# Cosine attention on one core: a second fold of the sums on GpSimd, and a new plan of loads and order

## The chip, the core and the metric

The kernel runs on one core of one Trainium2 chip. The core has TensorE (matmuls into PSUM), VectorE and ScalarE (both read PSUM and SBUF), GpSimd [...], and SyncE, which in this kernel issues nearly all transfers, one after the other, in the order of its program. Times are device microseconds of a whole execution. A page of the profile shows one execution; its span runs from the first to the last instruction. In the profile PE is TensorE, PEld its loads of stationary operands, DVE is VectorE, ACT ScalarE, POOL GpSimd, SP SyncE; SPq is SyncE's issuing of transfers.

## The reference

Attention with normalized queries and keys and one temperature for each head: 1 batch, 32 heads, 2048 positions, 20 elements a head, bfloat16.

```python
def reference(q, k, v, t):
    eps = 1e-6
    qn = q / (jnp.sqrt((q * q).sum(axis=-1, keepdims=True)) + eps)
    kn = k / (jnp.sqrt((k * k).sum(axis=-1, keepdims=True)) + eps)
    logits = jnp.einsum('bhqd,bhkd->bhqk', qn, kn) * t[None, :, None, None]
    attn = _softmax(logits, axis=-1)
    return jnp.einsum('bhqk,bhkd->bhqd', attn, v)
```

For each head 2048 x 2048 exponentials are needed, 134 million in all, and two matmuls with a depth or a width of only 20.

## The kernel before, in words

**Tiles.** The 2048 keys of a head are 16 row tiles of 128. For one row tile, TensorE makes the logits of 128 keys against all 2048 queries in four matmuls of 512 queries (`qk_mm`, line 758). Since the depth is 20, the queries of the four groups of 512 sit in four strips of 32 partitions, and the keys must be there in four rotations: `qkT` is the transposed tile, `kR` holds its three rotations, `qz` the queries, each in its own strip.

**Two ways to an exponential.** A row tile goes one of two ways. On way A, ScalarE computes the exponential from PSUM (`psA`) to `p_ring`, in waves of 2 and 3 units of 512 in turn (line 849; a unit is 128 keys by 512 queries). On way D, VectorE writes a scaled and shifted integer whose bits are a rough exponential (`xt`, line 905, two pieces of 1024 a row tile, both through the one buffer `psD`), and three more integers with 256, 512 and 768 added (`ss`, lines 912 and 916, called shifts here). The four, each with its own scaled copy of v (`vph`, line 574, made by GpSimd), average the error out. `DVE_TILES` says how many row tiles of each head go by way D; before, 157 of 512, and 355 by way A. A shift is either one VectorE instruction of 2048 int16 or GpSimd adds on pieces of it, seen as int32 (1024 words a shift). The products with v (line 778) add up in `psO`; the row sum comes from a column of ones in `vaug`. At the head's end VectorE transposes `psO` (line 791), takes the reciprocal, GpSimd multiplies (line 802), SyncE stores.

**Preparation of a head** (`add_loads`, `add_prep`, `add_trn`): SyncE loads k, q (four pieces) and v. VectorE squares (line 604), from head 3 on GpSimd adds the two halves of each row of 20 squares (`fold`, line 612, 320 elements a head), VectorE sums the rest (`rs_sum`, line 619) and finds the reciprocal root in five small steps (lines 623 to 635), multiplies the query half with the temperature (line 641). GpSimd normalizes (`qkn`, line 653; VectorE for heads 1 and 2). SyncE then issues a transposing transfer (line 671), which waits for that, four transfers into `qz` and six into `kR`. From head 5 on, two heads are prepared together. Only when `qz` and `kR` have landed can TensorE begin with the head.

**What sets the order.** A planner written in Python (`Program`) holds every instruction as a task with an engine, an assumed cost, a priority and its predecessors, and lists each engine's order once, when the program is built. On the chip each engine goes through its list, and waits for semaphores[...]. GpSimd's pieces are put into stretches in which VectorE runs an instruction of line 905, a reduction or a transpose (`pool_fill`, `win`). `schedule` lists anew up to `PASSES` times and chooses how many rows of the array a logit matmul uses (32, 64 or 128 partitions), to keep a measure of TensorE's activity above `LOAD`. `SWITCH` is an amount that a task of another kind on TensorE is put back by; `DSL` adds to the estimate of when VectorE is free; `SPARE` bounds which matmuls may be made wider. `LEAD` is how many heads ahead preparation is due, `SPREAD` how far its steps are set apart. `DLEAD` sets way D of a head 0.75 of a head ahead of way A. Three buffers (`NT`) hold transposed heads, so the transpose of head h waits until the logits of head h − 3 are made.

The DMA tasks have two costs in the planner: `dur`, how long SyncE's queue takes to issue one (0.65 if nothing is said), and `lat`, how long until it lands.

Of the kernel before, what the change touches and what calls it, by code (L numbers as in the profile page):

```python
# [45 lines left out]
class Program:  # L46
# [2 lines left out]

    SEM_LAT = {"PE": 0.20, "ACT": 0.30, "DVE": 0.14, "POOL": 0.15, "SP": 0.0}  # L50

    SWITCH = 0.1
    LIGHT = 9.0
    TICK = 3.41
    LOAD = 3550.0
    PASSES = 16
    FIRM = 8
    MARGIN = 600.0
    PE_REST = 4.2
# [2 lines left out]
    PRATE = 0.00164  # L62
    KEEP = 0.3
    RESTP = 0.3
    SPARE = 0.05
    DSL = 0.0
    HOLDA = 1.0
    HPE = 0.2
    HDV = 0.02
# [75 lines left out]
    def list_schedule(self):  # L145
# [39 lines left out]
        def leave(t, now):  # L185

            for u in t.users:
                lat = t.lat if t.dma else (
                    self.SEM_LAT[t.eng] if u.eng != t.eng else 0.12 if t.eng == "DVE" else 0.0)
                if u.eng == "PE" and u.name[:2] == "pv":  # L190
                    lat += self.PV_SLACK
                rt[u.seq] = max(rt[u.seq], t.end + lat)
                u.n -= 1
                if u.n == 0:
                    arrive(u, max(now, rt[u.seq]))
# [64 lines left out]
        while events or ready["POOL"]:  # L260
# [6 lines left out]
            while events and events[0][0] <= now:  # L267
                _, kind, _, t = heapq.heappop(events)
# [5 lines left out]
            for e in touched:  # L274
# [14 lines left out]
                if e == "PE":  # L289
# [8 lines left out]
                    t = x[2]  # L298
                elif e == "POOL":
# [3 lines left out]
                    t = x[2]  # L303
                else:
                    _, _, t = heapq.heappop(ready[e])
# [28 lines left out]
    def plan_waits(self):  # L334
        pos = {}
        for e, ts in self.order.items():
            for i, t in enumerate(ts):
                pos[t.seq] = i
        for t in self.tasks:
            for d in t.deps:  # L340
                if not d.dma and (d.eng != t.eng or d.eng == "DVE" or t.name == "qt0"):
                    d.inc = True
        dma_cnt = {}
        for e, ts in self.order.items():
            c = 0
            for t in ts:
                if t.dma:
                    dma_cnt[t.dma] = dma_cnt.get(t.dma, 0) + 16
                    t.cnt = dma_cnt[t.dma]
                elif t.inc:  # L350
                    c += 1
                    t.cnt = c
        allt = sorted(self.tasks, key=lambda t: (t.start, pos[t.seq]))
        known = {e: {} for e in self.order}
        snap = {}
        waits = {}
        for t in allt:
            kn = known[t.eng]
            need = {}
            for d in t.deps:  # L360
                if not d.dma and d.eng == t.eng and d.eng != "DVE" and t.name != "qt0":
                    continue
                key = d.dma if d.dma else d.eng
                if need.get(key, (0, None))[0] < d.cnt:
                    need[key] = (d.cnt, d)
            ws = []
            for key, (c, d) in sorted(need.items(), key=lambda kv: -kv[1][1].end):
                if kn.get(key, 0) >= c:
                    continue
                ws.append((key, c))  # L370
                kn[key] = c
                for k2, c2 in snap[d.seq].items():
                    if kn.get(k2, 0) < c2:
                        kn[k2] = c2
            waits[t.seq] = ws
            snap[t.seq] = dict(kn)
        self.waits = waits
# [12 lines left out]
def bass_standalone__qk_norm__prompt_kernel(  # L390
# [16 lines left out]
    NB = 8  # L407
# [8 lines left out]
    NWARM = 14  # L416
    EARLY = 3
    NSOLO = 3
    LEAD = 3.0
    SPREAD = 0.4  # L420
    FIRST = -7.0
    DLEAD = 0.75
    PE_MM = 0.23
    MORE = 12
    DLM = 2
    DVE_TILES = [4, 4, 4, 5, 4, 5, 5, 5, 5, 5, 5, 5, 5, 5, 6, 5, 6, 5, 5, 5, 5, 3, 5, 5, 5, 4, 5, 6, 6, 5, 5, 5]
    NDMAX = 6
    NPOOL, FPOOL = True, True
    FUSE, FOLD = True, 1
    NQ, NSQ, NSTEP = 2, 4, 0.0  # L430
    EXP0 = 0.051
    RSPOOL = False
    TTRATE = 0.00168
    TTDUR, TTWIN = 0.8, 0.55
    NCH = 1

    with ExitStack() as es:
# [14 lines left out]
        rs = {x: sbuf(f"rs_{x}", [128, 2 * NQ * R], F32) for x in ("sum", "u", "a", "b", "y", "r")}  # L452
# [19 lines left out]
        def dma(eng, name, dst, src, deps, pri, key, lat=2.2, dur=0.65):  # L472
            return add(eng, name, lambda e, tk: e.dma_start(dst, src), dur, deps, pri, lat=lat, dma=key)  # L473
# [59 lines left out]
        tcp = add("ACT", "tcp", lambda e, tk: e.activation(t_f32[:, :], tb16[:, :], ACT.Copy), 0.2, [ld_t], -90.85)  # L533


        lds, ld_v, norm, trn, rot = {}, {}, {}, {}, {}
# [14 lines left out]
        def add_loads(h):  # L551
            b, bv = (h + 1) % NB, h % NV
            pri = h - LEAD - 0.5
            war = (norm[h - NB] if h >= NB else []) + ([lambda: [trn[max(h - 3, 0) if h < 5 else h - 4]]] if h >= EARLY else [])
            x = qk_of(h)
            lds[h] = [dma("SP", f"ldk{h}", x[:, R:2 * R, :], k[0, h].rearrange("(p r) d -> p r d", p=128),
                          war, pri - 0.01 if h else -50, f"k{b}", lat=4.5 if h else 2.2)]
            if h == 0:
                lds[h].append(dma("ACT", "ldq0", x[:, 0:R, :], q[0, 0].rearrange("(p r) d -> p r d", p=128),
                                  [], -99, "q0a"))  # L560
            else:

                for nh in range(4):
                    src = bass.AP(q.tensor, q[0, h].offset + nh * D,
                                  [[16 * D, 32], [4 * D, 4], [512 * D, 4], [1, D]])
                    dst = x[32 * nh:32 * nh + 32, 0:R, :].rearrange("p (c g) d -> p c g d", g=4)
                    lds[h].append(dma("SP", f"ldq{h}", dst, src, war, pri, f"q{b}", lat=4.5))
            war = (pv_users[h - NV] if h >= NV else z_v[bv]) + ([lambda: [trn[h - 2]]] if h >= 2 else [])
            if h == 1:
                war = war + [lambda: [trn[0]]]  # L570
            ld_v[h] = dma("SP", f"ldv{h}", vaug[bv][:, :, 0:D], v[0, h].rearrange("(p r) d -> p r d", p=128),
                          war, pri + 0.1, f"v{bv}", lat=3.0)
            nd = 4 if h < DLM else DVE_TILES[h]
            vsc[h] = [add("POOL", f"vs{h}", lambda e, tk, i=i: e.tensor_scalar(  # L574
                vph[bv][:, i, 0:nd, :], vaug[bv][:, R - nd:R, :], 2.0 ** (-PHASES[i] / 1024.0), 1.0, ALU.mult, ALU.mult),
                0.4, [ld_v[h]] + (pv_users[h - NV] if h >= NV else z_v[bv]), pri + 0.2) for i in range(len(PHASES))]
            for u in vsc[h] if h else []:
                u.win = 0.14

        def add_prep(hs):  # L580
            due = hs[0] - LEAD if hs[0] != 1 else FIRST
            n = len(hs)
# [9 lines left out]
            def pool(name, fn, win, deps):  # L592
                step[0] += 1
                u = add("POOL", name + str(hs[0]), fn, win + 0.25, deps, due + SPREAD * (step[0] - 1) / 12)
                u.win = win
                return u
            parts = [(i, min(2, n - i)) for i in range(0, n, 2)] if FUSE and hs[0] > 2 else [(i, 1) for i in range(n)]
            for i, m in parts:
                h, m2 = hs[i], m * 2 * R
# [4 lines left out]
                c = [dv("sq", lambda e, tk, x=x, y=at[0][0]: e.tensor_tensor(y, x, x, ALU.mult), 0.065 + 0.3335 * m,  # L604
                        [u for k in range(m) for u in lds[h + k]] + [u for b in mine for u in sq_users.get(b, [])] +
                        (q0[2:] if h == 1 else []))]
                src, wd = at[0]
                nf = FOLD if h > 2 else 0
                for k in range(nf):
# [7 lines left out]
                    c = c2  # L617
                    src, wd = at[k + 1]
# [4 lines left out]
            c = dv("rs", lambda e, tk: e.tensor_scalar(  # L623
                rs["u"][:, 0:w].bitcast(I32), rs["sum"][:, 0:w].bitcast(I32), -0.5, RS_MAGIC, ALU.mult, ALU.add),
                0.065 + 0.033 * n, sums)

            def small(name, fn, deps):
                if RSPOOL and hs[0] > 2:
                    return pool(name, fn, 0.01 + 0.053 * 2 * n, deps)
                return dv(name, fn, 0.07 + 0.03 * n, deps)  # L630
            c = small("rs", lambda e, tk: e.tensor_tensor(rs["a"][:, 0:w], rs["u"][:, 0:w], rs["u"][:, 0:w], ALU.mult), [c])
            c = small("rs", lambda e, tk: e.tensor_tensor(rs["b"][:, 0:w], rs["a"][:, 0:w], rs["sum"][:, 0:w], ALU.mult), [c])
            c = small("rs", lambda e, tk: e.scalar_tensor_tensor(
                rs["y"][:, 0:w], rs["b"][:, 0:w], RS_K1, rs["b"][:, 0:w], ALU.add, ALU.mult), [c])
            c = small("rs", lambda e, tk: e.scalar_tensor_tensor(
                rs["r"][:, 0:w], rs["y"][:, 0:w], RS_K0, rs["u"][:, 0:w], ALU.add, ALU.mult), [c])
            rq = rs["r"][:, 0:w].rearrange("p (n x) -> p n x", n=n)[:, :, 0:R]
            tq = t_f32[:, hs[0]:hs[0] + n]
            tq = bass.AP(tq.tensor, tq.offset, [tq.ap[0], [1, n], [0, R]])
            if hs[0]:  # L640
                c = small("rs", lambda e, tk: e.tensor_tensor(rq, rq, tq, ALU.mult), [c, tcp])
            if hs[0] == 0:
                first_head(c)
                prep_last[0] = norm[0] + head0[-1:]
# [364 lines left out]
```

## Time and profile before

| | |
|---|---|
| median of 3 runs | 661.57 us (661.47 to 661.71) |
| span of the profiled execution | 660.4 us, TensorE's mean granted clock 0.995 |
| exponentials on ScalarE (line 849) | 568 instructions, 642.5 us: 284 of 1536 (1643 ns), 284 of 1024 (1223 ns) |
| way D on VectorE (line 905) | 314 instructions, 381.9 us, 1216 ns each |
| shifts on VectorE (line 912) | 352, 234.5 us, 681 ns each |
| shifts on GpSimd (line 916) | 335 pieces, 322.5 us |
| sums on VectorE (line 619) | 13 of 640 elements (806 ns), 3 of 320 (453 ns), 3 unfolded |
| folds on GpSimd (line 612) | 29, 28.5 us, 982 ns each |
| normalizing on GpSimd (line 653) | 29, 47.6 us, 1641 ns each |

How to read the views. The busy line gives each engine's busy time and its share of the span. A line of the waits view reads: engine and line that waited, what released it, us in total, how many times, the longest. A line of the timeline reads: start, duration, engine, line, instruction with what it writes and reads, how many alike in a row, and in brackets how long the engine had stood before it and what let it go. Instructions of VectorE overlap a little at their ends in the records, so that what one costs in a full stretch is the time from its start to the start of the next: an xt at 40.80 us is followed at 41.93.

### The profile page before, as it was taken

How to read it: one execution, taken by the hardware profiler on the slowest of the kernel's cores; microseconds unless marked ns; L12 is line 12 of the kernel's file. 1: busy time of each engine (PE TensorE's matmuls, PEld its weight loads, DVE VectorE, ACT ScalarE, POOL GpSimd, SP SyncE). 2: the span in 40 equal slices, each digit the busy share in tenths (PEclk: the TensorE clock that was granted, in tenths of full speed). 3: DMA queues.
4: the chain of work that ended last, by engine and by line, in shares of the span. 5: the costliest groups of instructions: out<-in, count | busy, mean ns of one | idle time of the engine just before them, and what ended most of it. 6: DMA issues, size and time to landing. Idle time of an engine off the chain costs nothing.

```text
span 660.4 us, 14800 instructions
## 1 busy us (share of the span) xinstructions
PE 591.1 (90%) x5979; PEld 168.0 (25%) x6007; DVE 645.3 (98%) x902; ACT 649.7 (98%) x577; POOL 469.2 (71%) x542
## 2 busy tenths in 40 slices
PE   7887898888999888998989999899999889999997
PEld 2221222222222222222222222222222222222222
DVE  8998899999999999999999999999999999999997
ACT  9998899999999999999999999999999999999997
POOL 2675775678677877787777778787687865877652
PEclk9999899999999999999999999999999999999999
DMA  5544334343441524425235242452423424140200
GB/s 64 81 62 72 62 38 86 44 76 45 70 70 21 88 30 74 63 33 86 21 67 69 43 80 20 67 70 41 85 22 85 47 52 75 33 77 6 55 6 11
DMA packets 196724, 36.25 MB, mean 55 GB/s; under 512 B 172592, under 2 KB 196656, under 8 KB 196656
## 3 DMA queue, kind: packets, MB, share of 16 engines
q1 hardware_dynamic: 196512, 35.22, 34.9%
q8 instruction: 47, 0.77, 0.5%
q14 instruction: 21, 0.17, 0.1%
q10 hardware_dynamic: 144, 0.08, 0.1%
HBM read 7.87 MB, written 2.62 MB: 16 GB/s over the span
## 4 chain that ended last, share of the span: by engine, by line
ACT 81%; DVE 14%; PE 2%; SPq 1%; issue 1%; DMA 1%; POOL 0%; DVEq 0%
ACT p_ring L849 81%; DVE xt L905 7%; DVE ss L912 4%; SPq L473 1%; PE psO L685 1%; DMA kR<-qkT 1%; DVE rs_sum L619 1%; PE psO L778 1%; DVE sq L604 0%; DVE oT L791 0%; PE psD L758 0%; PE psA L758 0%; DVE qkn L660 0%; DVE qz L729 0%; DVE o_stage L802 0%
## 5 line engine op out<-in xcount | busy, mean ns | idle before, releaser
L849 ACT ACTIVATE p_ring<-psA 128x1024 bf16<-128x1024 f32 (+1 forms) x568 | 642.5, 1433 | 5.1 <-PE psA L758 5.0
L916 POOL TENSOR_TENSOR ss<-xt,add_w 128x672 int32<-128x672 int32 (+14 forms) x335 | 322.5, 969 | 110.5 <-DVE ss L912 58.0
L905 DVE TENSOR_SCALAR xt<-psD 128x1024 int16<-128x1024 f32 x314 | 381.9, 1216 | 9.2 <-PE psD L758 7.9
L758 PE MATMUL psA<-qz,kR 32*128 32x512 bf16 (+2 forms) x1048 | 218.6, 386 | 43.9 <-ACT p_ring L849 39.5
L912 DVE TENSOR_SCALAR ss<-xt 128x2048 int16<-128x2048 int16 x352 | 234.5, 681 | 0.3
L778 PE MATMUL psO<-ss,vph 128*32 128x512 f16 x1884 | 166.6, 386 | 0.0
L758 PE MATMUL psD<-qz,kR 64*128 64x512 bf16 (+1 forms) x466 | 121.0, 386 | 8.7 <-DVE xt L905 4.8
L758 PE MATMUL psA<-qz,qkT 32*128 32x512 bf16 (+2 forms) x350 | 115.8, 386 | 10.1 <-ACT p_ring L849 8.4
L778 PE MATMUL psO<-p_ring,vaug 128*32 128x512 bf16 x1420 | 124.3, 386 | 0.1
L758 PEld LDWEIGHTS psA<-qz,kR 32*128 32x128 bf16 (+2 forms) x1065 | 53.0, 92 | 180.9 <-ACT p_ring L849 179.7
L574 POOL TENSOR_SCALAR vph<-vaug 128x160 f16<-128x160 bf16 (+3 forms) x96 | 40.6, 423 | 32.5 <-DMA vaug<-in_v_dram 13.1
L778 PE MATMUL psO<-xt,vaug 128*32 128x512 f16 x628 | 62.4, 387 | 0.0
L778 PEld LDWEIGHTS psO<-ss,vph 128*32 128x32 f16 x1884 | 42.6, 94 | 69.8 <-issue 58.2
L758 PE MATMUL psD<-qz,qkT 64*128 64x512 bf16 (+1 forms) x156 | 59.1, 387 | 1.3 <-DVE xt L905 0.7
L653 POOL TENSOR_TENSOR qkn<-qk_sb,rs_r 128x640 bf16<-128x640 bf16 x29 | 47.6, 1641 | 14.3 <-DVE ss L912 5.0
L758 PEld LDWEIGHTS psD<-qz,kR 64*128 64x128 bf16 (+1 forms) x471 | 29.9, 93 | 71.3 <-DVE xt L905 44.3
L778 PEld LDWEIGHTS psO<-p_ring,vaug 128*32 128x32 bf16 x1420 | 32.6, 94 | 58.2 <-issue 48.9
L758 PEld LDWEIGHTS psA<-qz,qkT 32*128 32x128 bf16 (+2 forms) x355 | 27.9, 92 | 55.6 <-ACT p_ring L849 54.3
L802 POOL TENSOR_TENSOR o_stage<-oT,rec 128x320 bf16<-128x320 f32 x30 | 28.4, 946 | 14.7 <-DVE ss L912 7.1
L612 POOL TENSOR_TENSOR fold<-sq 128x320 f32<-128x320 bf16 x29 | 28.5, 982 | 9.4 <-DVE ss L912 5.8
L791 DVE STREAM_TRANSPOSE oT<-psO 128x512 f32<-128x512 f32 x32 | 22.6, 705 | 1.2 <-PE psO L778 1.0
L778 PEld LDWEIGHTS psO<-xt,vaug 128*32 128x32 bf16 x628 | 16.3, 94 | 28.1 <-issue 22.1
(48 smaller groups left out, 102.4 us busy)
## 6 DMA issues: line engine op xcount, KB each, us to landing
kR<-qkT SPq DMA_DIRECT2D x62, 96.0 KB, 2.1
qz<-qkT SPq DMA_DIRECT2D x124, 32.0 KB, 1.8
kR<-qkT SPq DMA_DIRECT2D x62, 64.0 KB, 2.0
qk_sb<-in_k_dram SPq DMA_DIRECT2D x32, 80.0 KB, 2.7
vaug<-in_v_dram SPq DMA_DIRECT2D x32, 80.0 KB, 3.6
qk_sb<-in_q_dram SPq DMA_DIRECT2D x124, 20.0 KB, 2.6
out_dram<-o_stage SPq DMA_DIRECT2D x31, 80.0 KB, 3.0
kR<-qkT SPq DMA_DIRECT2D x62, 32.0 KB, 1.9
```

Source lines behind the costliest of these rows:

```text
L473: return add(eng, name, lambda e, tk: e.dma_start(dst, src), dur, deps, pri, lat=lat, dma=key)
L574: vsc[h] = [add("POOL", f"vs{h}", lambda e, tk, i=i: e.tensor_scalar(vph[bv][:, i, 0:nd, :], vaug[bv][:, R - nd:R, :], 2.0 ** (-PHASES[i] ...
L612: c2.append(pool("fold", lambda e, tk, a=a, k=k, at=at: e.tensor_tensor(at[k + 1][0][:, a:a + 2 * R, :], at[k][0][:, a:a + 2 * R, 0:at[k + ...
L653: u = add("POOL", f"norm{h}", lambda e, tk, x=x, b=b, i=i, j=j: e.tensor_tensor(qkn[b][:, j:j + m, 0:D], x[:, j:j + m, :], bc(rs["r"][:, 2 ...
L758: return eng.matmul(dst, lhsT, mov, tile_position=(p0, 0))
L778: last = eng.matmul(psO[32 * g:32 * g + 32, :], w, rhs_of(g), start=start, stop=False, skip_group_check=True, tile_position=(0, 32 * g))
L791: trO[h] = add("DVE", f"tr{h}", lambda e, tk: e.transpose(oT[:, :, :].rearrange("p r d -> p (r d)"), psO[:, :]), 0.63, [lambda: pv_users[h ...
L802: fin[h] = add("POOL" if pool else "DVE", f"fin{h}", lambda e, tk: e.tensor_tensor(st, src, rb, ALU.mult), TTDUR if pool else 0.40, [rc] + ...
L849: act[w] = add("ACT", f"exp{w}", lambda e, tk: e.activation(p_ring[:, p0 * 512:p0 * 512 + n], psA[:, slot * WAVES[0] * 512:slot * WAVES[0] ...
L905: t1_prev[nchunk[0]] = add("DVE", f"t1.{j}.{k}", lambda e, tk, o=o, slot=slot: e.tensor_scalar(xt[sx][:, o:o + W1], psD[:, slot * W1:slot ...
L912: f = add("DVE", f"s{i}.{js[0]}", lambda e, tk, i=i, dst=dst: e.tensor_scalar(dst[:, be:be + w], xt[0][:, bx:bx + w], float(PHASES[i]), No ...
L916: f.alt = lambda c, n, i=i, dst=dst: lambda e, tk: e.tensor_tensor(dst[:, be + 2 * c:be + 2 * (c + n)].bitcast(I32), xt[0][:, bx + 2 * c:b ...
```

## The change

The sums are folded a second time: after the fold from 20 to 10, GpSimd adds the halves once more, from 10 to 5 (29 folds of 160 elements), and VectorE's reduction reads half as many. The second fold reads what the first wrote on the same engine, so the planner now gives GpSimd waits on its own semaphore. A path is added by which the temperature product can run on GpSimd (`RTPOOL`, which is False here), and a term by which the load gate of more early heads can be put later (`LGATE`, which is 0 here). The planner's costs are refined: a k load takes the queue 0.5, a q load 0.68, a v load 1.4; the v load's priority is put back by 0.3 instead of 0.1. Several planner settings change, the way D tiles are spread over the heads otherwise and are 158, and the order is planned anew with them. The purpose is to take reduction work off VectorE, to let GpSimd do more, and to have the loads planned nearer to what they take. Shortened to what matters (line numbers after it are 3 to 4 higher than before):

```diff
-    SWITCH = 0.1
+    SWITCH = 0.4
-    PASSES = 16
+    PASSES = 20
-    SPARE = 0.05
-    DSL = 0.0
+    SPARE = 0.0
+    DSL = 0.1
...
-                    self.SEM_LAT[t.eng] if u.eng != t.eng else 0.12 if t.eng == "DVE" else 0.0)
+                    self.SEM_LAT[t.eng] if u.eng != t.eng or t.eng == "POOL" else 0.12 if t.eng == "DVE" else 0.0)
...
-                if not d.dma and (d.eng != t.eng or d.eng == "DVE" or t.name == "qt0"):
+                if not d.dma and (d.eng != t.eng or d.eng in ("DVE", "POOL") or t.name == "qt0"):
...
-                if not d.dma and d.eng == t.eng and d.eng != "DVE" and t.name != "qt0":
+                if not d.dma and d.eng == t.eng and d.eng not in ("DVE", "POOL") and t.name != "qt0":
...
-    LEAD = 3.0
-    SPREAD = 0.4
+    LEAD = 3.2
+    SPREAD = 0.5
-    DVE_TILES = [4, 4, 4, 5, 4, 5, 5, 5, 5, 5, 5, 5, 5, 5, 6, 5, 6, 5, 5, 5, 5, 3, 5, 5, 5, 4, 5, 6, 6, 5, 5, 5]
+    DVE_TILES = [4, 4, 4, 5, 4, 5, 5, 5, 5, 5, 5, 5, 5, 5, 6, 5, 5, 6, 5, 5, 3, 5, 5, 5, 6, 5, 4, 6, 5, 5, 6, 5]
-    FUSE, FOLD = True, 1
+    FUSE, FOLD = True, 2
+    RTPOOL = False
+    VPRI = 0.3
+    LGATE = 0
...
-            war = (norm[h - NB] if h >= NB else []) + ([lambda: [trn[max(h - 3, 0) if h < 5 else h - 4]]] if h >= EARLY else [])
+            war = (norm[h - NB] if h >= NB else []) + ([lambda: [trn[max(h - 3, 0) if h < 5 + LGATE else h - 4]]] if h >= EARLY else [])
...
-                          war, pri - 0.01 if h else -50, f"k{b}", lat=4.5 if h else 2.2)]
+                          war, pri - 0.01 if h else -50, f"k{b}", lat=4.5 if h else 2.2, dur=0.5)]
...
-                    lds[h].append(dma("SP", f"ldq{h}", dst, src, war, pri, f"q{b}", lat=4.5))
+                    lds[h].append(dma("SP", f"ldq{h}", dst, src, war, pri, f"q{b}", lat=4.5, dur=0.68))
...
-                          war, pri + 0.1, f"v{bv}", lat=3.0)
+                          war, pri + VPRI, f"v{bv}", lat=2.6, dur=1.4)
...
-                c = small("rs", lambda e, tk: e.tensor_tensor(rq, rq, tq, ALU.mult), [c, tcp])
+                f = lambda e, tk: e.tensor_tensor(rq, rq, tq, ALU.mult)
+                c = pool("rs", f, 0.02 + 0.027 * n, [c, tcp]) if RTPOOL and hs[0] > 2 else small("rs", f, [c, tcp])
```

## The prediction

> **What bounds the kernel now.** I read the busy shares first, then the waits of the two fullest engines, then the one place where both stand still.
>
> ```profile
> PE 591.1 (90%) x5979; PEld 168.0 (25%) x6007; DVE 645.3 (98%) x902; ACT 649.7 (98%) x577; POOL 469.2 (71%) x542
> PEclk9999899999999999999999999999999999999999
> ...
> DVE xt L905 <- PE psD L758: 7.9, 11, 3.2
> ...
> ACT p_ring L849 <- PE psA L758: 5.0, 5, 2.8
> PE psD L758 <- DMA kR<-qkT: 3.0, 1, 3.0
> ```
>
> VectorE and ScalarE are both at 98%: neither can give work to the other for nothing. ScalarE's waits for data are five, 5.0 us together. Stage by stage they lie in one spot (columns: stretch, its length, then busy us of PE, weight load, VectorE, ScalarE, GpSimd, and the granted clock):
>
> ```profile
> 60.00:72.00 12.00, 9.01 (x77) 1.94 (x69) 6.89 (x12) 7.16 (x7) 4.16 (x5) 0.72 0.54 68
> 542.00:552.00 10.00, 9.42 (x102) 2.78 (x101) 8.14 (x12) 10.00 (x10) 3.17 (x5) 1.00 0.31 77
> 123.00:656.00 533.00, 487.72 (x5039) 139.19 (x5060) 528.26 (x713) 532.81 (x472) 395.19 (x435) 1.00 0.33 53
> ```
>
> Between 60 and 72 us ScalarE loses 4.84 us and VectorE 5.11; TensorE's clock falls to 0.72. From 123 to 656 us ScalarE has no gap above 0.2 us, VectorE lacks 4.7 us of 533: there ScalarE is the bound by a little. At 548 us VectorE alone waits (1.82 us in three waits). The cause of the first hole is in the order of time:
>
> ```profile
> 46.06 1.59 POOL L653 TENSOR_TENSOR qkn<-qk_sb,rs_r 128x640 bf16<-128x640 bf16 x1 [0.29 <-DVE rec L794]
> 48.88 0.63 SPq L473 DMA_DIRECT2D qk_sb<-in_k_dram  x1
> 49.55 1.26 SPq L473 DMA_DIRECT2D qk_sb<-in_q_dram  x2
> 50.85 1.37 SPq L671 DMA_TRANSPOSE qkT<-qkn  x1
> ...
> 54.97 2.53 SPq L473 DMA_DIRECT2D qz<-qkT  x4
> 57.54 3.77 SPq L473 DMA_DIRECT2D kR<-qkT  x6
> ...
> 64.73 0.61 PE L758 MATMUL psD<-qz,kR 64*128 64x512 bf16 x2 [2.99 <-DMA kR<-qkT]
> 65.38 1.23 DVE L905 TENSOR_SCALAR xt<-psD 128x1024 int16<-128x1024 f32 x1 [3.25 <-PE psD L758]
> 65.81 1.02 ACT L849 ACTIVATE p_ring<-psA 128x1024 bf16<-128x1024 f32 x1 [2.80 <-PE psA L758]
> ```
>
> Head 3's normalized q and k are ready at 47.65, but its transpose is issued at 50.85: 3.2 us in which SyncE's in-order queue still issues loads of later heads. The rotated keys kR land at 64.7; TensorE, in order too, has stood since 61.7, and behind that matmul stand those for ScalarE. Then matmuls take 0.61 us instead of 0.39 until 71 us, which gives three more short waits.
>
> [...]
>
> **The change part by part.** The counts are from the order of instructions that the two builds give. Where instructions follow closely, the cost is from start to start: 1.13 us for an xt (40.80 to 41.93), 0.60 for a shift ss. RTPOOL is False and LGATE 0: the temperature product stays on VectorE and the load gate is unchanged, both cost nothing because they are not in the program.
>
> 1. *One more VectorE tile* (158 instead of 157): +2 xt = +2.3 us. ScalarE loses 4 of 1420 units: one activation of 1024 and one of 1536 go, one of 512 comes. A pair of 5 units takes 532.55/1178 x 5 = 2.26 us (471 activations with 1178 units from 123.63 on); the 512 comes to some 0.5. So ScalarE −1.8 us.
> 2. *Second fold.* 13 sums shrink from 640 to 320 elements, 3 from 320 to 160: by the two reduce rows (806 and 453 ns, 0.35 for 320 elements) 13 x 0.35 + 3 x 0.17 = −5.0 us. GpSimd gets 29 folds of 160 elements. This shape isn't in the trace; nearest below is an add of 160 int32 (523 ns), above the present fold (982). I take 0.55: +16 us (15 to 28). GpSimd has 29% free, and its pieces sit inside xt windows.
> 3. *Shifts back to VectorE.* The windows that the folds take are lost to shifts: GpSimd's add-words fall from 121,856 to 117,760, that is 4 whole shifts; with 3 of the extra tile, VectorE's shifts go from 352 to 359: 7 x 0.60 = +4.2 us.
> 4. *VectorE's sum*: 2.3 − 5.0 + 4.2 = +1.5 us.
> 5. *Self-waits on GpSimd.* Behind a fold waiting for the first one stand GpSimd's shifts and norms, and VectorE's sum waits for it. In the order of after, between the point of VectorE that releases the second fold and the sum lie at least 1.74 us (an xt and a shift); a fold begins some 0.3 us after release and takes 0.5 to 1.0. So nothing, at worst 16 x 0.1.
> 6. *The planned costs of the loads, V later, LEAD 3.2.* These move instructions only. In SyncE's new order, between head 2's rotations and head 3's transpose stand q, q, V, k, q, q instead of q, V, k, q x4, k, q, q, and one q fewer before head 2's rotations. At the trace's costs (k 1.40, V 0.64, q 0.7 to 0.98) the queue reaches the transpose at about 47.0 instead of 50.85, and the norm isn't late: VectorE's order releases it 16.5 us of work ahead of head 3's first xt (16.0 before), so it ends near 46.2. From a free transpose to the first kR takes 6.4 us (91.89 to 98.35 for head 5), to the last 10.2: issued by 57.5, landed by 60, needed at 61.7. The hole at 60 to 72 goes: −4.84 for ScalarE, −5.11 for VectorE.
> 7. *The other tight heads.* I count VectorE's work between the release of a norm and its head's first xt: the chain to the last kR took 11.85 us (90.28 to 102.13, head 5) and a further 1.8 must pass until the xt, 13.65 in all. Before: head 5 15.6 and head 25 14.8, no wait; head 27 13.8, with the 1.82 us at 548, where a transpose waiting for TensorE stood in the queue ahead of qz. After: heads 4 and 27 14.8, head 5 15.6, all others over 16. No hole there; head 27 still has that transpose ahead, 0 to 0.5 us left of 1.82.
>
> The sums: ScalarE 660.4 − 4.84 − 0.2 − 1.8 = 653.6 us of span if nothing holds it. VectorE 660.4 − 5.11 − 1.82 + 1.5 = 655.0 with all its other small idle kept; in the stretch 123 to 656 it had 2.9 us of such idle because ScalarE held it, so part of that can go. I take 654.9 of span. The runs are 1.2 us over the span (661.57 against 660.4): **656.1 us**, 0.8% less.
>
> **The rivals.**
> *A, ScalarE alone binds*: VectorE fills all its idle; 653.6 + 1.2 = 654.8. For: between 123 and 656 it was so. Against: VectorE's own demand rises 1.5 while ScalarE's falls 1.8.
> *B, the hole shrinks or moves*: kR of head 3, 4 or 27 still comes late by half as much, and half of the clock's slump stays: 656.1 + 2.5 = 658.6. For: loads of about 11 us now stand between head 3's last kR and head 4's transpose (two k, eight q, V, one store), which puts that transpose at 65 to 68 us, just where its norm ends (68). Against: 14.8 us of lead.
> *C, slower*: no gain in the early heads, since GpSimd's longer fold chain (at 1 us each, in order, with self-waits) delays a norm as much as the queue did; the hole stays elsewhere and the demand of VectorE comes on top: 661.57 + 1.5 = 663.1. For: heads 4, 9, 11 and 29 have less lead than before. Against: the slack of item 5, and 29% idle GpSimd.
>
> **How the numbers follow.** Main case 0.60, A 0.15, B 0.16, C 0.06, and 0.03 for a loss of all gains without a new cost, about 661. The low end is A with 0.4 us off for the tail; the high end lies past B by 1.2 us, so that only C and the worst of B is left out: 654.4 to 659.8. Faster by over 0.2% means under 660.2: main, A and nearly all of B, 0.88; same 0.05; slower 0.07.
>
> **What would show it.** In the trace after: the transpose of head 3 issued near 47 us; no wait of TensorE for kR over 0.5 us; clock 1.0 in the slice at 60 to 72; VectorE's sums 128x64 near 0.46 us, x359 ss, 316 xt; ScalarE's waits under 2 us in all; no wait of VectorE for GpSimd. It would be wrong if VectorE's rows themselves got longer[...], if the second fold took over 1.4 us, or if a new wait for kR or qz at heads 4, 5 or 27 stopped both engines.

## The result, and the profile after

The changed kernel takes **655.25 us** (median of 4 runs, 654.74 to 655.75) against 661.53 us before in the same session: ratio 0.9905, 95% interval 0.9887 to 0.9922. The forecast was 656.1 us, range 654.4 to 659.8. Executions of the kernel before fall into two groups, which matters below: in the sessions of the experiments 77 of 85 took 660.2 to 663.1 us with a mean granted clock of 0.997 or less, the other 8 took 657.3 to 659.2 with 0.999 or 1.0; its median and its profile are of the larger group.

First the busy line and the granted clock of the kernel after, from its page:

```profile
span 654.0 us, 14865 instructions
...
PE 590.3 (90%) x5991; PEld 168.9 (26%) x6019; DVE 646.1 (99%) x911; ACT 647.4 (99%) x576; POOL 472.7 (72%) x550
...
PEclk9999999999999999999999989999999999999999
```

No engine does much less: VectorE 0.8 us more, ScalarE 2.3 us less, GpSimd 3.5 us more. The span is 6.4 us shorter, so most of that came out of idle time. The stages of the kernel after (stretch, length, then busy us of PE, weight load, VectorE, ScalarE, GpSimd, clock):

```profile
...
60.00:72.00 12.00, 11.05 (x124) 3.21 (x122) 12.00 (x21) 12.00 (x12) 8.63 (x10) 1.00 0.52 58
542.00:552.00 10.00, 9.31 (x108) 2.71 (x104) 10.00 (x14) 10.00 (x10) 7.15 (x10) 1.00 0.60 81
```

Where ScalarE had 7.16 us of 12 and VectorE 6.89, both now have all 12, with the clock at 1.00; the three VectorE waits near 548 us are gone too. The lines of the early heads that answer to those of before, in the order of time:

```profile
43.77 1.66 POOL L657 TENSOR_TENSOR qkn<-qk_sb,rs_r 128x640 bf16<-128x640 bf16 x1
43.99 1.28 SPq L476 DMA_DIRECT2D qk_sb<-in_k_dram  x1
45.31 1.27 SPq L476 DMA_DIRECT2D qk_sb<-in_q_dram  x2
46.62 2.15 SPq L675 DMA_TRANSPOSE qkT<-qkn  x1
...
51.76 2.50 SPq L476 DMA_DIRECT2D qz<-qkT  x4
54.30 3.78 SPq L476 DMA_DIRECT2D kR<-qkT  x6
...
60.30 1.23 DVE L909 TENSOR_SCALAR xt<-psD 128x1024 int16<-128x1024 f32 x1
```

Head 3's norm ends at 45.43, its transpose is issued at 46.62 (50.85 before), the last rotation at 58.08 (61.31 before), and head 3's first xt at 60.30 has no bracket: it waited for nothing. But it is close. TensorE's two matmuls for that xt start at 59.87; the last rotation lands at 59.62:

```profile
59.87 0.39 PE L762 MATMUL psD<-qz,kR 64*128 64x512 bf16 x2
```

ScalarE's exponentials, in the kernel before (first and last row of its six) and in the kernel after (two unbroken rows with one gap of 0.93 us):

```profile
8.66 54.35 ACT L849 ACTIVATE p_ring<-psA 128x1024 bf16<-128x1024 f32 x48
...
123.63 532.55 ACT L849 ACTIVATE p_ring<-psA 128x1536 bf16<-128x1536 f32 x471 [0.19 <-PE psA L758]
```

```profile
8.42 371.68 ACT L853 ACTIVATE p_ring<-psA 128x1024 bf16<-128x1024 f32 x329
381.03 268.62 ACT L853 ACTIVATE p_ring<-psA 128x1536 bf16<-128x1536 f32 x238 [0.93 <-PE psA L762]
```

Read as a sum, ScalarE accounts for both spans:

| us of the span | before | after |
|---|---|---|
| first exponential starts | 8.66 | 8.42 |
| waits between exponentials | 5.03 | 0.93 |
| exponentials, start of the first to end of the last, less waits | 642.49 | 640.30 |
| from the end of the last to the end | 4.22 | 4.35 |
| span | 660.4 | 654.0 |

Of the 6.4 us, 4.1 are waits and 2.2 are exponentials; the start is 0.2 earlier and the end 0.1 longer. The one gap left ends a spell at half clock (0.50 granted from 378 to 381 us) ahead of which TensorE had not stood for more than 0.53 us; what brings such a spell stays open. A second profile of the changed kernel (see the last group of experiments) has no gap at all and a span of 653.5. The chain of work of the kernel after says the same in one line: it is ScalarE from beginning to end.

```profile
ACT 97%; PE 2%; DVE 0%; issue 0%; ACTq 0%
```

### The profile page after: what moved, and what is told of

The parts are those of the page before. It is cut to its first block, busy times and chain, and to the rows that moved or that the text cites. A ratio compares the mean times of both kernels' runs of the same rounds, so it can differ in the third digit from the quotient of the medians.

```text
span 654.0 us, 14865 instructions
## 1 busy us (share of the span) xinstructions
PE 590.3 (90%) x5991; PEld 168.9 (26%) x6019; DVE 646.1 (99%) x911; ACT 647.4 (99%) x576; POOL 472.7 (72%) x550
## 3 DMA queue, kind: packets, MB, share of 16 engines
HBM read 7.87 MB, written 2.62 MB: 16 GB/s over the span
## 4 chain that ended last, share of the span: by engine, by line
ACT 97%; PE 2%; DVE 0%; issue 0%; ACTq 0%
ACT p_ring L853 96%; PE psO L782 1%; PE psA L762 1%; ACT qz L529 0%; ACT L518 0%; PE psD L762 0%; ACT qz L730 0%; DVE oT L795 0%; ACT xq L697 0%; DVE o_stage L806 0%; ACTq L476 0%; ACT qkT L725 0%; DVE rec L798 0%; ACT act_scr L518 0%; ACT t_f L536 0%
## 5 line engine op out<-in xcount | busy, mean ns | idle before, releaser
L909 DVE TENSOR_SCALAR xt<-psD 128x1024 int16<-128x1024 f32 x316 | 384.8, 1218 | 2.8 <-PE psD L762 1.5
L920 POOL TENSOR_TENSOR ss<-xt,add_w 128x672 int32<-128x672 int32 (+16 forms) x314 | 311.4, 999 | 102.3 <-DVE ss L916 57.8
L762 PE MATMUL psA<-qz,kR 32*128 32x512 bf16 (+2 forms) x1045 | 215.5, 386 | 40.4 <-ACT p_ring L853 33.5
L916 DVE TENSOR_SCALAR ss<-xt 128x2048 int16<-128x2048 int16 x359 | 239.1, 681 | 0.0
L782 PE MATMUL psO<-ss,vph 128*32 128x512 f16 x1896 | 169.7, 385 | 0.0
L782 PE MATMUL psO<-p_ring,vaug 128*32 128x512 bf16 x1416 | 127.8, 385 | 0.0
L762 PE MATMUL psA<-qz,qkT 32*128 32x512 bf16 (+2 forms) x349 | 114.3, 385 | 9.9 <-ACT p_ring L853 8.1
L782 PEld LDWEIGHTS psO<-p_ring,vaug 128*32 128x32 bf16 x1416 | 34.2, 94 | 56.9 <-issue 48.1
```

What stands on the lines that cost most here:

```text
L762: return eng.matmul(dst, lhsT, mov, tile_position=(p0, 0))
L782: last = eng.matmul(psO[32 * g:32 * g + 32, :], w, rhs_of(g), start=start, stop=False, skip_group_check=True, tile_position=(0, 32 * g))
L909: t1_prev[nchunk[0]] = add("DVE", f"t1.{j}.{k}", lambda e, tk, o=o, slot=slot: e.tensor_scalar(xt[sx][:, o:o + W1], psD[:, slot * W1:slot ...
L916: f = add("DVE", f"s{i}.{js[0]}", lambda e, tk, i=i, dst=dst: e.tensor_scalar(dst[:, be:be + w], xt[0][:, bx:bx + w], float(PHASES[i]), No ...
L920: f.alt = lambda c, n, i=i, dst=dst: lambda e, tk: e.tensor_tensor(dst[:, be + 2 * c:be + 2 * (c + n)].bitcast(I32), xt[0][:, bx + 2 * c:b ...
```

## The experiments

All changes of order were made on the planner's finished lists, so that every other engine's list stayed as it was, except where it says "planned anew". Times are medians; the kernel before had 661.46, 661.36 and 660.96 us in the three sessions. Differences under half a microsecond between sessions are not read.

### Is the early hole the gain? Its cure in the kernel before, its return in the kernel after

In the kernel before, four loads of head 6 go behind head 3's rotations (directly ahead of that head's fifth), and two q loads of head 5 behind head 3's transpose:

```diff
         prog.schedule()
+        sp = prog.order["SP"]
+        late = lds[6][:4]
+        for u in late:
+            sp.remove(u)
+        last = lds[6][4]
+        at = sp.index(last)
...
+        sp[at:at] = late
+        q5 = lds[5][3:5]
+        t3 = trn[3]
+        for i, u in enumerate(q5):
+            sp.remove(u)
...
+        at = sp.index(t3) + 1
+        sp[at:at] = q5
         prog.plan_waits()
```

> The kernel before with one edit: in the transfer queue, the loads of head 6 are put behind head 3's rotations and two q loads of head 5 behind head 3's transpose; all other engines' orders are the same. My theory (the late rotations of head 3 are the larger part of the gain): transpose issued near 47.7 us instead of 50.85, last rotation issued near 58.7 instead of 61.3, ScalarE's wait between 60 and 72 us falls from 4.84 us to under 0.6, span 655.4 to 656.0, time about 656.8 (ratio 0.993). Rival (the gain is VectorE's smaller sums and the new order; the hole was slack that VectorE or the end would have taken anyway): span above 658.5, ratio above 0.996, with new waits of 2 us or more elsewhere.

Measured: 657.88 us (657.47 to 658.22), ratio 0.9947 [0.9932, 0.9962], so 3.6 us of the change's 6.3. All six runs lie in the range of the smaller group of the kernel before. In its trace the transpose is at 49.03 and the rotations are issued by 60.19, 1.3 and 1.5 us later than I had expected; TensorE's stop for kR shrinks from 2.99 to 0.27 us, ScalarE's waits from 5.0 to 1.2. Its trace in the order of time, with rows of the transfer queue, TensorE and VectorE:

```profile
56.41 3.78 SPq L473 DMA_DIRECT2D kR<-qkT  x6
61.77 0.39 PE L758 MATMUL psD<-qz,kR 64*128 64x512 bf16 x2 [0.27 <-DMA kR<-qkT]
62.20 1.23 DVE L905 TENSOR_SCALAR xt<-psD 128x1024 int16<-128x1024 f32 x1 [0.31 <-PE psD L758]
```

And ScalarE's waits of the same run (sum in us, how many, the longest):

```profile
ACT p_ring L849 <- PE psA L758: 1.2, 4, 0.6
```

The VectorE wait at head 27 is untouched here (1.1 us, the longest of its xt waits), and ScalarE has no gap there: that wait cost the exponentials nothing.

How much of the hole is the place in the queue? The view of the rotations of the kernel before between 55 and 72 us, and of this run, shows when they landed:

```profile
L473 SPq DMA_DIRECT2D kR<-qkT x6: 578/594/598, 57.5 to 60.7; - x6
...
DMA to landing us min/median/max: 1.9/2.0/4.0
```

```profile
L473 SPq DMA_DIRECT2D kR<-qkT x6: 590/594/602, 56.4 to 59.6; - x6
...
DMA to landing us min/median/max: 1.9/2.0/2.2
```

In the profile of before the last of the six copies took 4.0 us to land; the same copy took 2.12 to 2.15 in the twelve other profiles. Some 1.8 us of the stop of 2.99 are that late landing, and a stop of about 1.2 us would have been left without it (an estimate from these landings). So the move in the queue, which brings the last copy's issue forward by only 1.1 us, cures more than itself: the late landing and the half clock are gone too. Whether the old order makes the late landing, or only has no margin for one, these runs don't tell.

In the kernel after, the five loads of head 6 go ahead of head 3's transpose. That is more than a return: in the kernel before only three of them stood there, and eleven loads, not ten, now lie between head 2's rotations and that transpose:

```diff
         prog.schedule()
+        sp = prog.order["SP"]
+        t3 = trn[3]
+        late = lds[6]
+        for u in late:
+            sp.remove(u)
+        at = sp.index(t3)
...
+        sp[at:at] = late
         prog.plan_waits()
```

> The changed kernel with one edit: the five loads of head 6 are put ahead of head 3's transpose in the transfer queue, as they stood before. My theory: the transpose comes some 4 us later (near 51 us), TensorE stands for about 3.5 us, its clock falls, ScalarE loses 4.5 to 6.5 us between 60 and 74, and the time is 4 to 6 us above that of the changed kernel, 659.5 to 661. Rival (the place of this transpose is hidden by other slack in the new order): under 1.5 us above it.

Measured: 660.42 us, 5.2 above the changed kernel, from this one move. Its transpose is at 52.35 (50.85 in the kernel before), its last rotation is issued by 63.01 (61.31); the hole is back in its old place. ScalarE's rows of its trace:

```profile
60.59 2.53 ACT L853 ACTIVATE p_ring<-psA 128x1536 bf16<-128x1536 f32 x2 [0.36 <-PE psA L762]
65.74 2.37 ACT L853 ACTIVATE p_ring<-psA 128x1536 bf16<-128x1536 f32 x2 [2.62 <-PE psA L762]
69.33 585.06 ACT L853 ACTIVATE p_ring<-psA 128x1536 bf16<-128x1536 f32 x518 [1.23 <-PE psA L762]
```

The 2.62 us is the stop itself; the 1.23 behind it came with the lower clock (0.75 granted between 60 and 72 us). In this run matmuls took about 0.6 us already from 55.9 to 62, before the stop, so 1.0 us of the 4.9 us of waits isn't the stop's. Cure and return agree in direction, 3.6 us gained one way and 5.2 lost the other; the sizes needn't be equal, since this move goes further than the old order. That the place of five or six loads around head 3's transpose alone is worth several microseconds is shown; what the landing and the clock add to it is only read from the traces.

### Which engine binds after? A little work added to each

Ten small instructions that nobody waits for, spread over the whole kernel after, on one engine at a time:

```diff
+        fill_s = sbuf("fill_s", [128, 192], BF16)
...
         prog.plan_waits()
+        mine = [u for u in prog.order["ACT"] if u.name[:3] == "exp"]
+        for u in mine[60::56]:
+            u.fn = lambda e, tk, f=u.fn: (e.activation(fill_s[:, :], ones[:, 0:192], ACT.Copy, scale=0.0), f(e, tk))[1]
```

> The changed kernel with ten added ScalarE instructions (zeros from ones to an unused tile of 192 elements, about 0.2 us each) ahead of every 56th exponential, 2.1 us in all. Rival A of the prediction (ScalarE alone binds): the time goes up by all of it, 1.8 to 2.3 us. My main case (ScalarE and VectorE bind by turns): up by 1 us or less.

Measured: 657.83 us, 2.6 above the changed kernel. Each added instruction is recorded with 523 ns on average, but overlaps its neighbours; from its start to the start of the next it takes 0.26 us, 2.6 in all, and all of it arrives at the end:

```profile
77.12 0.35 ACT L962 ACTIVATE fill_s<-ones 128x192 bf16<-128x192 bf16 x1
77.38 2.35 ACT L854 ACTIVATE p_ring<-psA 128x1024 bf16<-128x1024 f32 x2
```

```diff
+        fill_s = sbuf("fill_s", [128, 192], F32)
...
         prog.plan_waits()
+        mine = [u for u in prog.order["DVE"] if u.name[:2] == "t1"]
+        for u in mine[33::31]:
+            u.fn = lambda e, tk, f=u.fn: (e.memset(fill_s[:, :], 0.0), f(e, tk))[1]
```

> The changed kernel with ten added VectorE instructions (a memset of an unused tile of 192 float32, about 0.2 us each) ahead of every 31st xt, 2 us in all. If ScalarE alone binds and VectorE has about 3 us of idle left in the middle: up by under 0.5 us. If VectorE binds as well, as in my main case: up by 1 us or more.

Measured: 655.37 us, 0.1 above. The group is there in its profile, ten of 218 ns:

```profile
L962 DVE MEMSET fill_s<- 128x192 f32 x10 | 2.2, 218 | 0.0
```

So ScalarE alone binds in this order, though both engines are at 99%. VectorE had room for two more microseconds.

### What is the second fold worth?

The plan of the kernel after kept, but VectorE's sums read the first fold again:

```diff
-                sums.append(dv("sum", lambda e, tk, i=i, m2=m2, src=src: e.tensor_reduce(
+                sums.append(dv("sum", lambda e, tk, i=i, m2=m2, src=at[1][0] if nf == 2 else src: e.tensor_reduce(
```

> The changed kernel with the order untouched, but VectorE's 16 sums read the first fold (10 wide) instead of the second (5 wide): VectorE gets the 5.0 us back that the second fold took from it, GpSimd still makes both folds. Theory (ScalarE binds; VectorE had some 3 us of room, of which 2 were already shown to be free): up by 0.5 to 2.5 us. Rival (the fold's 5 us on VectorE are worth their full size): up by 4 to 5 us. Second rival (VectorE has room for all of it): within 0.4 us.

Measured: 655.88 us, 0.6 above the changed kernel. The groups of its sums, then those of the kernel after:

```profile
L622 DVE TENSOR_REDUCE rs_sum<-fold 128x64 f32<-128x640 f32 x13 | 10.5, 806 | 0.0
...
L622 DVE TENSOR_REDUCE rs_sum<-fold 128x32 f32<-128x320 f32 x3 | 1.4, 473 | 0.0
```

```profile
L622 DVE TENSOR_REDUCE rs_sum<-fold 128x64 f32<-128x320 f32 x13 | 6.1, 472 | 0.0
...
L622 DVE TENSOR_REDUCE rs_sum<-fold 128x32 f32<-128x160 f32 x3 | 0.9, 305 | 0.0
```

That is 4.9 us of VectorE's time back, and nearly all of it disappears in idle time.

One fold, planned anew:

```diff
-    FUSE, FOLD = True, 2
+    FUSE, FOLD = True, 1
```

> The changed kernel with one fold instead of two, everything else as changed, planned anew: 16 sums are wider (+5.0 us on VectorE), but 10 shifts go from VectorE to GpSimd (349 instead of 359, -6.0 us), since the windows are free for them; VectorE's total is 1 us less. Head 3's transpose stands behind one load more than in the changed kernel. Theory (the fold only swaps sums against shifts on VectorE; ScalarE binds): within 1.5 us of the changed kernel. Rival (the second fold is what made it faster): up by 3 us or more without a hole in the early heads.

Measured: 657.64 us, 2.4 above the changed kernel: neither case. ScalarE goes through without a gap,

```profile
9.31 640.25 ACT L853 ACTIVATE p_ring<-psA 128x1024 bf16<-128x1024 f32 x567
```

and ends at 649.56, as in the kernel after (649.65). The loss lies behind that: VectorE's last shifts run to 651.3 and GpSimd's last piece from 650.80 to 651.95, and the end comes 6.5 us after the last exponential instead of 4.35. VectorE also waited 2.4 us at head 5 (104.6 us), where its lead had been counted at 14.4 us. Which of the two brings the late tail, the wait or the wider sums, this run doesn't tell. Four of its 20 runs took 660.3 us and more at a mean granted clock of 0.993 to 0.997; those were not profiled.

The fold and GpSimd's self-waits alone in the kernel before, planned anew with the old settings:

```diff
-                if not d.dma and (d.eng != t.eng or d.eng == "DVE" or t.name == "qt0"):
+                if not d.dma and (d.eng != t.eng or d.eng in ("DVE", "POOL") or t.name == "qt0"):
...
-    FUSE, FOLD = True, 1
+    FUSE, FOLD = True, 2
```

> The kernel before with the second fold and GpSimd's waits on itself alone, planned anew with the old settings: 157 tiles, VectorE's shifts 361 instead of 352. In the new plan head 3's transpose happens to stand three loads further ahead than before, and comes near 48.9 us instead of 50.85. Theory (the place of that transpose is the gain, the fold itself is none, ScalarE binds): the hole shrinks to 0.5 to 2 us of ScalarE's time, and the time is 657 to 659, as when only the transfer queue was rearranged. Rival (the fold is a gain of its own): under 656.5.

Measured: 659.44 us, with 20 runs between 656.96 and 660.6; the profile is of the quickest of them, and has the transpose at 47.95 and no hole (0.48 us of wait on VectorE). The median is above the 657 to 659 that I had expected. Eleven of the runs are at 659.2 us and more with a mean granted clock of 0.996 or 0.997, nine at 658.4 and less with 0.999 or 1.0: the slower ones come with the lower clock, as most executions of the kernel before do, but none of them was profiled. The best run is 0.5 us below the rearranged queue's best, so these runs show no clear gain of the fold's own in the old plan. They do show that planning anew around the second fold, with the old costs of the loads, put head 3's transpose 2.9 us earlier.

### The switch that the change leaves off

```diff
-    RTPOOL = False
+    RTPOOL = True
```

> The changed kernel with the temperature product put on GpSimd, which the change names but leaves switched off; planned anew. 16 small VectorE instructions go (-1.9 us), but the windows that they take from the shifts bring VectorE's shifts from 359 to 366 (+4.2). The norm of head 5 is released only 11.6 us of VectorE's work ahead of that head's first xt, where about 13.65 are needed. Theory: a hole of 2 to 4 us at head 5, and 1 us more from VectorE's sum: 658 to 661. Rival (ScalarE alone counts): within 1 us of the changed kernel.

Measured: 664.36 us, 9.1 above the changed kernel; the only version slower than the kernel before (ratio 1.0056 [1.0035, 1.0078]). The hole at head 5 is where the count of leads put it:

```profile
106.20 1.23 DVE L909 TENSOR_SCALAR xt<-psD 128x1024 int16<-128x1024 f32 x1 [3.66 <-PE psD L762]
108.03 1.23 DVE L909 TENSOR_SCALAR xt<-psD 128x1024 int16<-128x1024 f32 x1 [0.60 <-PE psD L762]
```

But the size is off, since ScalarE didn't lose by it: its exponentials end at 650.6. VectorE does: it makes the last head's xt until 656.3 and its shifts until 658.3, and the end comes 11.8 us after the last exponential. Here VectorE ends last: 7 more shifts (366) and 4.3 us of waits were too much for it. That this sum makes the whole 9.1 us isn't shown.

### A tile more

Since ScalarE binds and VectorE has room, 159 tiles instead of 158, the planner's cost of an exponential as the trace has it, planned anew; two spreads over the heads:

```diff
-    SWITCH = 0.4
+    SWITCH = 0.7
...
-    DVE_TILES = [4, 4, 4, 5, 4, 5, 5, 5, 5, 5, 5, 5, 5, 5, 6, 5, 5, 6, 5, 5, 3, 5, 5, 5, 6, 5, 4, 6, 5, 5, 6, 5]
+    DVE_TILES = [4, 4, 4, 5, 5, 5, 5, 5, 5, 5, 4, 6, 6, 5, 5, 5, 5, 5, 6, 5, 3, 5, 5, 6, 6, 5, 4, 5, 5, 5, 6, 5]
...
-    EXP0 = 0.051
+    EXP0 = 0.063
...
```

That is the first. The second keeps SWITCH, has EXP0 the same, wider margins of the planner (LEAD 3.3, SPREAD 0.6), other values of KEEP, DSL, DLEAD and VPRI, and this spread:

```diff
+    DVE_TILES = [4, 4, 4, 5, 5, 4, 5, 5, 5, 5, 6, 5, 5, 5, 6, 6, 3, 6, 4, 6, 5, 5, 4, 4, 6, 5, 5, 6, 5, 5, 6, 5]
...
```

> The changed kernel with one tile more on VectorE (159), spread anew over the heads, the planner's cost of an exponential raised by 0.012 us to what the trace shows, and a few settings moved (SWITCH 0.7, KEEP 0.4, DSL 0, SPREAD 0.4, VPRI 0.5). ScalarE loses four more units (-1.8 us); VectorE gets about 2.3 us of work more, and has shown 2 to 4 us of room. Theory (ScalarE alone binds): 653.4 to 654.6 us, faster than the changed kernel by about 1.3. Rival (VectorE's room is used up, or its end sets the tail): no faster than the changed kernel, or up to 2 us slower, with ScalarE done over 5 us before the end.

> As the version before it, 159 tiles with another spread over the heads and other settings (LEAD 3.3, SPREAD 0.6, DLEAD 0.7, KEEP 0.5, DSL 0.3). The norm of head 23 is released 14.1 us of VectorE's work ahead of that head's first xt, that of head 17 14.8: by the count that held so far (13.65 needed) no hole, or one under 0.5 us. 653.4 to 655.0 us.

> The changed kernel once more, to be compared with the two versions beside it: 655.3 to 655.8 us.

Measured in one session: the changed kernel 655.07 (654.75 to 655.38), the first spread 654.25 (653.33 to 654.91), the second **653.74** (653.15 to 655.1). The second's row of ScalarE's exponentials:

```profile
8.88 638.44 ACT L853 ACTIVATE p_ring<-psA 128x1024 bf16<-128x1024 f32 x565
```

And the longest of VectorE's waits in it, which is the one for the last products:

```profile
DVE oT L795 <- PE psO L782: 1.2, 1, 1.2
```

Against 640.19 us in the changed kernel's profile of that session, ScalarE is 1.75 us shorter, which is what four units cost; the time follows by 1.3. One of its six runs lies within the range of the changed kernel, and other settings moved with the tile, so the step is likely and small (0.2%), and whether it is the tile's alone isn't shown. Heads 17 and 23, with 14.8 and 14.1 us of lead, show no wait.

## Why the prediction was right, point by point

**The hole (items 6 and 7).** Right in place and nearly in size. Forecast: transpose at 47.0, last kR issued by 57.5 and landed by 60, 4.84 us back for ScalarE. Measured 46.62, 58.08 and 59.62; the 4.84 us at 60 to 72 are gone entirely, and the two experiments put the place of this transpose at 3.6 and 5.2 us. Two parts of the reasoning were weaker than the number. The prediction laid the whole stop to the queue, and some 1.8 us of it were the late landing. And it took the moment of need, 61.7, from the kernel before: after the change TensorE asks at 59.87, so that 0.25 us of margin are left and not 1.7. In two profiles of the same order with work added (`a_dve_more`, `a_sum_wide`) the last copy landed at 60.4 and 60.5 and head 3's first xt waited 0.60 and 0.51 us. That the hole closed completely was in part luck. In the kernel before, the clock was granted at 0.50 from 66 to 70 us, behind the stop of 2.99 us, and was at half for some 6.9 us (an estimate from 0.57 granted between 64 and 72 us). That the stop brought it isn't shown: two traces have half clock with no such stop ahead of it, `after` (0.50 granted from 378 to 381 us, no stop over 0.53 us in the 20 us ahead) and `a_trn3_late` (matmuls of about 0.6 us from 55.9 us on, ahead of its stop). Heads 4, 5 and 27 show no wait for kR; head 27, given 0 to 0.5 us, has none, and its last kR is issued 2.1 us ahead of its first xt.

**ScalarE's four units (item 1).** Forecast −1.8. The exponentials' stretch is 2.2 us shorter in one profile and 2.3 in the other; a tile more, with other settings moved too, gives 1.75 again. The rest is within what the same 567 instructions vary by, 640.2 to 641.0 us in the profiles of this order with its waits taken out (`after`, `after_again`, `a_sum_wide`).

**VectorE's sum (items 2 to 4).** Forecast +1.5; busy time +0.8. The reduce rows came out at 472 ns for 320 elements and 305 for 160, against 806 for 640 and 453 for 320 (473 in `a_sum_wide`) with one fold: 0.33 and 0.15 to 0.17 us saved each, 0.35 and 0.17 taken. The xt rows stayed at 1218 ns (1216), so GpSimd's added pieces did not lengthen them.

**The second fold and the self-waits (items 2 and 5).** I took 0.55 us between bounds of 0.52 and 0.98; the row says 597 ns, 17.3 us in all. Shifts on GpSimd fell by 11.1 us (322.5 to 311.4). No wait of VectorE for GpSimd appears. Right. The row of the second fold:

```profile
L615 POOL TENSOR_TENSOR fold<-fold 128x160 f32<-128x160 f32 x29 | 17.3, 597 | 2.6 <-DVE ss L916 1.6 <-DVE xt L909 0.9
```

**Which engine sets the end.** This is the step that was off, within the range: I gave 0.60 to a case in which VectorE's small idle stays and holds ScalarE (654.9 us of span) and 0.15 to rival A, ScalarE alone (653.6). The added work on each engine settles it for A. The spans are 654.0, with a gap of 0.93, and 653.5 without one. I had read from 123 to 656 us that ScalarE had no gap while VectorE lacked 4.7 us of 533, and then didn't draw the conclusion: the idle time of VectorE, which ScalarE held, was room: 2.2 us more work there cost 0.1 (`a_dve_more`). It cost 0.9 us of forecast. The room has an end: 4.9 us more cost 0.6 (`a_sum_wide`).

**Rivals B and C** did not come about: the hole didn't move, and the fold chain delayed no norm that counted. Experiments show that a hole was near: one load group out of place costs 5.2 us, and a lead of 11.6 us at head 5 gives a wait of 3.7 us, where 2 to 4 had been expected.

**What the change's name promised.** Of its four parts, the new place of a few transfers in SyncE's queue is the larger one, the extra tile by way D the smaller; the second fold is worth 0.6 us with the order kept, and up to 2.4 where the order was planned anew around a single one, and the temperature product and the later gate aren't in the program. Which of the new settings moved the transfers isn't separated: LEAD, SWITCH, the spread of the tiles, the loads' costs and the fold were never changed one at a time, except the fold. The new costs are not all nearer to the trace: a v load is planned with 1.4 us, and in the kernel before it held the queue 0.60 to 1.35 us, 0.62 in the median.

## What to carry to other kernels

Two engines at 98 or 99% need not be two bounds (here 2.6 us added to ScalarE cost 2.6, 2.2 added to VectorE cost 0.1): look for the one whose row of instructions has no gap, and add a little idle work to each to be sure. Where one queue issues its transfers in the order of a list, as SyncE's does here (a few loads moved in that list were worth 3.6 and 5.2 us), ask of each critical transfer what is issued between the moment its data is ready and its turn; loads that nobody needs soon belong behind it. Count the work between a release and its first use in the order lists before and after a change: a lead of 11.6 us gave a wait of 3.7. But the count alone isn't enough: one of 14.4 had 2.4 us of wait, and head 3 of the kernel before had 3.25 with a lead of 16.0, because of what stood in the transfer queue and when the last copy landed.

## What the runs showed of the hardware beyond what was expected

- The same load takes the queue very different times: a k load of 80 KB 0.39 to 1.78 us within the trace of after, an 80 KB store 0.33 to 2.37. A planner with one cost for each will be wrong by over a microsecond at single loads; how much of the hole of before that made isn't shown.
- The last of a head's six copies of rotated keys mostly lands 2.1 us after its issue, but now and then late (12 of the 186 copies of all heads took over 2.7 us in the trace of after): 4.0 us for the last one of head 3 in the kernel before, 3.9 for the last one of head 9 in the kernel after, where nothing waited for it.
- The first exponential starts between 8.41 and 9.31 us in profiles of programs whose beginnings are alike. The spread of whole runs depends on the plan: the single fold's 20 runs go from 656.96 to 662.05, the changed kernel's ten from 654.74 to 655.75. That the margin at head 3 makes the difference would fit, and isn't shown.
- TensorE's clock was at half without a stop, too: 0.50 granted from 378 to 381 us in the kernel after (longest stop in the 20 us ahead 0.53 us), and from 56 to 60 us in `a_trn3_late`, at 3.86 us busy of 4.
- A ScalarE instruction of 192 elements was recorded with 523 ns on average but delayed the next by 0.26 us (`a_act_more`).
